# Expert layers of a routed network on one core: every third first-layer block in a third PSUM bank, and the next expert's weights converted in 14 small pieces

## The chip, the core and the metric

The kernel runs on one core of a Trainium2 chip. Its work is spread over the engines PE (TensorE, the matrix unit; its weight loads are listed apart as PEld), ACT (ScalarE), DVE (VectorE), POOL (GpSimd) and SP (SyncE, which here only issues transfers). The metric is the device time of one execution in microseconds (us). The kernel before takes 799.66 us, the median of three runs (799.56 to 800.76).

## What is computed

Three stages follow each other: a recurrent attention, a dense feed-forward layer, and a layer of eight experts. The change lies in the last one alone. Each of the 3072 tokens is given to one of 8 experts, 384 tokens to each, and passes through that expert's two matrices:

```
def _moe2_ref(x, w_gate, w1, w2):          # x 3072 x 384, w1 8 x 384 x 1024, w2 8 x 1024 x 384
    ...                                    # assigned[token] = expert, 384 tokens for each
    for e in range(E):
        mask = assigned == e
        h = np.maximum(x[mask] @ w1[e], 0.0)
        out[mask] = h @ w2[e]
```

## The kernel before

All matrices of the expert stage are multiplied as sums of f16 halves: a number is scaled and rounded to f16 (its high half), and what is left goes into a second f16 tile (its low half). A product of two such numbers takes three matmuls: high by high, high by low, low by high.

**One expert.** The loop over experts (L1223 to L1240) does the following for expert e.

- First layer, `e_mm1` (L1142 to L1163): the 1024 hidden features are cut into 8 blocks of 128. A block is 9 matmuls of 128 x 128 by 128 x 384 (3 slices of the 384 inputs, 3 products of halves each) into one PSUM tile `Hp`. ACT then writes the high half of its ReLU to `hT` (L1162), and DVE, which reads the same PSUM tile and ACT's result, writes the low half (L1163). Only after DVE has read it can the PSUM tile be filled again. `Hp` has two buffers, of one bank each, so block f waits until DVE is through with block f - 2. In expert 0 blocks 0 and 1 are worked on together, in three parts of 128 tokens, since their inputs come late.
- Behind each of the blocks 0 to 5 one step of the conversion of the next expert's weights is issued, `conv_w` (L1106): ACT writes the high half of a part of the staged f32 weights to `a` (L1101), DVE the low half (L1104). `halves` (L1089) sets the parts: three of 1024 elements per partition for w1, then two of 1152 and one of 768 for w2. Both tiles come from the staging tile `stg`, which SP fills for the expert after (L1084 for w1, L1086 for w2) as soon as DVE has read it.
- With block 0 POOL fetches the next expert's rows by index (`gather`, L1125).
- Second layer, `e_mm2` (L1168): three blocks of 128 tokens, 24 matmuls each (L1175). Ahead of each, PE transposes 128 of the next expert's rows (L1137), and ACT and DVE write their halves to `xe` (L1139, L1140). ACT scales the result (L1178) and POOL scatters it to the output (L1180).

Each engine takes its instructions in the order in which the program issues them, so on ACT and DVE the conversion of a part stands between the ReLU of a block and that of the next one. Expert 0's own weights are converted earlier, during the routing, by `small_pieces` (L1111): w1 in 6 pieces of 512 elements and w2 in 8 pieces of 384. The last expert, 7, has no weights to convert.

[...]

Of the kernel before, what the change touches and what calls it, by code (L numbers as in the profile page):

```python
# [9 lines left out]
F32 = mybir.dt.float32  # L10
# [8 lines left out]
P = 128  # L19
# [4 lines left out]
CFG = {'conv': [-28.559, -28.796, -9.197, -0.926, 0.696, 1.907, 2.814, 4.759, 2.932, 5.667, 6.934, 7.118, 8.281, 10.201,  # L24
          10.159, 10.891],
 'split': [-27.728, -26.98, -0.788, 1.233, 2.549, 2.564, 3.442, 5.926, 5.381, 6.383, 8.239, 9.176, 8.901, 10.848,
           10.815, 11.802],
 'ogT': [6.61, 8.484, 9.185, 9.828, 11.404, 11.777, 11.841, 12.734],
 'ogM': [8.421, 8.977, 10.284, 11.259, 11.757, 11.949, 12.856, 14.904],
 'u': ({'att0': -3.966,  # L30
        'bon1': -2.332,
        'bon2': -0.558,
# [122 lines left out]
 'alone': {9},  # L155
 'lg': 8.068,
 'hold': 30,
 'xq': set()}


@with_exitstack
def tile_rwkv_mish_greedy_moe(
# [17 lines left out]
    NE = w_gate.shape[1] * P // DM  # L180
# [11 lines left out]
    CAP = NT // NE  # L192
# [24 lines left out]
    pp = ctx.enter_context(tc.tile_pool(name="psm", bufs=1, space=PSUM))  # L217
# [560 lines left out]
    p_g2, p_g3, pgs = cms["g2"], cms["g3"], cms["ps"]  # L778
# [301 lines left out]
    NCV = KD + 3  # L1080

    def load_w(e):
        s1 = p2.tile([P, KD, F2], F32, name="stg")
        nc.sync.dma_start(s1.rearrange("p k f -> p (k f)"), w1[e])  # L1084
        s2 = p2.tile([P, NF2, DM], F32, name="stg")
        nc.sync.dma_start(s2.rearrange("p f d -> p (f d)"), w2[e])  # L1086
        wts[e] = (s1, s2)

    def halves(e, step):  # L1089
        s1, s2 = wts[e]  # L1090
        if step == 0:
            wf[e] = tuple(p2b[e % 2].tile(sh, F16, name=nm, bufs=1)
                          for sh, nm in (([P, 2, KD, F2], "a1"), ([P, 2, NF2, DM], "a2")))
        a1, a2 = wf[e]
        if step < KD:
            return s1[:, step], a1[:, :, step], SW1
        h = slice(3 * (step - KD), min(3 * (step - KD) + 3, NF2))
        return s2[:, h], a2[:, :, h], SW2

    def conv_hi(src, dst, sc_):  # L1100
        nc.scalar.activation(dst[:, 0], src, AF.Copy, scale=sc_)  # L1101

    def conv_lo(src, dst, sc_):
        nc.vector.scalar_tensor_tensor(dst[:, 1], src, sc_, dst[:, 0], op0=ALU.mult, op1=ALU.subtract)  # L1104

    def conv_w(e, step):  # L1106
        x = halves(e, step)
        conv_hi(*x)
        conv_lo(*x)

    def small_pieces(e):  # L1111
        for step in range(NCV):
            src, dst, sc_ = halves(e, step)
            if step < KD:
                for q in range(2):
                    c = slice(q * F2 // 2, (q + 1) * F2 // 2)
                    yield src[:, c], dst[:, :, c], sc_
            else:
                for q in range(src.shape[1]):
                    yield src[:, q], dst[:, :, q], sc_  # L1120

    def gather(e):
        for m in range(ME):
            t = xe[e, m] if (e, m) in xe else p3.tile([P, DM], F32, name="xr", bufs=4)
            nc.gpsimd.indirect_dma_start(  # L1125
                out=t, out_offset=None, in_=x1_dram[:, :],
                in_offset=bass.IndirectOffsetOnAxis(ap=idx[:, e * ME + m:e * ME + m + 1], axis=0))
            xe[e, m] = t

    def xpose(e, m):  # L1130
        if m == 0:
            xe[e] = p3.tile([P, 2, KD, CAP], F16, name="xe")
        x = xe[e]
        t = xe.pop((e, m))
        ps = pgs.tile([P, KD, P], F32, name="cn")
        for kk in range(KD):
            nc.tensor.transpose(ps[:, kk, :], t[:, kk * P:(kk + 1) * P], ident)  # L1137
        ms = slice(m * P, (m + 1) * P)
        nc.scalar.activation(x[:, 0, :, ms], ps, AF.Copy, scale=SX1)  # L1139
        nc.vector.scalar_tensor_tensor(x[:, 1, :, ms], ps, SX1, x[:, 0, :, ms], op0=ALU.mult, op1=ALU.subtract)  # L1140

    def e_mm1(e, *fs, parts=1):  # L1142
        a1, x = wf[e][0], xe.get(e)
        if 0 in fs:
            hT[e] = p3.tile([P, 2, NF2, CAP], F16, name="hT")
        h = hT[e]
        tiles = [pp.tile([P, CAP], F32, name="Hp", bufs=2) for _ in fs]
        for c in range(parts):
            cs = slice(c * CAP // parts, (c + 1) * CAP // parts)
            if parts > 1:  # L1150
                for m in range(c and c + 1, min(c + 2, parts)):
                    xpose(e, m)
                x = xe[e]
            for f, ps in zip(fs, tiles):
                n = 0
                for kk in range(KD):
                    for a, b in ((0, 0), (0, 1), (1, 0)):
                        nc.tensor.matmul(ps[:, cs], a1[:, a, kk, f * P:(f + 1) * P], x[:, b, kk, cs],  # L1158
                                         start=(n == 0), stop=(n == 3 * KD - 1))
                        n += 1  # L1160
        for f, ps in zip(fs, tiles):
            nc.scalar.activation(h[:, 0, f], ps, AF.Relu)  # L1162
            nc.vector.scalar_tensor_tensor(h[:, 1, f], ps, 0.0, h[:, 0, f], op0=ALU.max, op1=ALU.subtract)  # L1163
# [4 lines left out]
    def e_mm2(e, m):  # L1168
        a2, h = wf[e][1], hT[e]
        ps = pp.tile([P, DM], F32, name="X", bufs=2)  # L1170
        ms = slice(m * P, (m + 1) * P)
        n = 0
        for f in range(NF2):
            for a, b in ((0, 0), (0, 1), (1, 0)):
                nc.tensor.matmul(ps, h[:, a, f, ms], a2[:, b, f, :], start=(n == 0), stop=(n == 3 * NF2 - 1))  # L1175
                n += 1
        o = p3.tile([P, DM], F32, name="or", bufs=3)
        nc.scalar.activation(o, ps, AF.Copy, scale=1.0 / (SX1 * SW1 * SW2))  # L1178
        nc.gpsimd.memset(spacer, 0.0)  # L1179
        st_ = nc.gpsimd.indirect_dma_start(  # L1180
            out=out[:, :], out_offset=bass.IndirectOffsetOnAxis(ap=idx[:, e * ME + m:e * ME + m + 1], axis=0),
            in_=o, in_offset=None)
        for s_ in scat:
            tc.declare_no_dep(st_.ins, s_.ins, reason="each row is written once")
        scat.append(st_)
# [33 lines left out]
    if CFG["hold"]:  # L1219
        hold = pgs.tile([P, P], F32, name="cn")  # L1220
        for _ in range(CFG["hold"]):
            nc.tensor.matmul(hold[:, 0:P], ones, OH[:, 0], start=True, stop=True)  # L1222
    for e in range(NE):  # L1223
        nx = e + 1 < NE
        f = 0
        while f < NF2:
            k = 2 if e == 0 and f == 0 else 1
            e_mm1(e, *range(f, f + k), parts=ME if k > 1 else 1)
            for i in range(f, f + k):
                if i == 0 and nx:  # L1230
                    gather(e + 1)
                    if e > 0:
                        load_w(e + 1)
                if nx and i < NCV:
                    conv_w(e + 1, i)
            f += k
        for m in range(ME):
            if nx:
                xpose(e + 1, m)
            e_mm2(e, m)  # L1240
# [73 lines left out]
```

## Time and profile before

| | us |
|---|---|
| median of the runs | 799.66 |
| the profiled execution | 801.9 |
| its span, first to last instruction | 800.2 |
| PE busy | 748.7 (94%) |
| DVE busy | 546.7 (68%) |
| ACT busy | 457.3 (57%) |
| POOL busy | 58.7 (7%) |
| the expert stage in the span | 583.8 to the end |

The page of the profile cuts the span into 40 equal slices and gives the busy share of each engine in tenths. PE stands at 9 nearly throughout; the dip to 6 and 8 just behind the middle of the second half is the routing. Busy shares are averages over the span, and a PE that is 94% busy can still wait in one stage; that is read from the timeline of the stage, in which a bracket behind a row says how long the engine was idle before it and what ended the wait. Durations of matmuls include the time in the pipeline: a matmul of 384 columns shows 326 ns, though they follow each other more closely.

### The profile page before, as it was taken

What the parts mean: (1) busy time and instruction counts of PE and PEld (TensorE: products, weight loads), DVE (VectorE), ACT (ScalarE), POOL (GpSimd) and SP (SyncE); (2) the same over time, 40 slices, a digit from 0 to 9 for tenths busy, and PEclk for the clock granted to TensorE, in tenths of its full rate; (3) what the DMA queues carried; (4) which work ended last, traced back from release to release, by engine and by line L of the source; (5) the groups of instructions that cost most, each with busy time, mean ns of one, the idle gap of its engine ahead of it and who ended that gap; (6) DMA issues with size and microseconds to landing.
All of it is one profiled execution on the core that took longest, in us unless ns stands there. A gap on an engine that the chain in (4) does not pass through costs nothing. (4 is left out here: it accounts for less than half of the span.)

```text
span 800.2 us, 20251 instructions
## 1 busy us (share of the span) xinstructions
PE 748.7 (94%) x8848; PEld 519.3 (65%) x8848; DVE 546.7 (68%) x962; ACT 457.3 (57%) x711; POOL 58.7 (7%) x98
## 2 busy tenths in 40 slices
PE   5877789999999999999999999999689999999996
PEld 3465576877778777787877765555466555555563
DVE  7899995978879778796974556777653455335520
ACT  4369989686786877869686761110053455435521
POOL 0000000000000000000000010000112122312211
PEclk9799889999999999999999999999879999999999
DMA  9860521313223132231200032004224554355100
GB/s 342 247 187 19 157 71 27 72 44 77 51 56 81 28 84 53 56 81 27 52 16 16 2 124 75 22 11 137 77 86 160 198 196 146 127 184 207 50 30 29
DMA packets 22220, 74.12 MB, mean 93 GB/s; under 512 B 4496, under 2 KB 13072, under 8 KB 20080
## 3 DMA queue, kind: packets, MB, share of 16 engines
q1 hardware_dynamic: 19056, 63.35, 26.6%
q0 software_dynamic: 3072, 9.44, 3.7%
q8 instruction: 71, 1.16, 0.6%
q14 instruction: 21, 0.17, 0.1%
HBM read 62.15 MB, written 9.44 MB: 89 GB/s over the span
## 5 line engine op out<-in xcount | busy, mean ns | idle before, releaser
L570 PE MATMUL Hp<-xg,wi 128*128 128x256 f16 x1728 | 208.4, 277 | 0.4 <-DMA xg<-xg 0.3
L625 PE MATMUL X<-wo,g 128*128 128x392 f16 (+1 forms) x1152 | 208.4, 328 | 0.0
L570 PEld LDWEIGHTS <-wi 128*128 128x128 f16 x1728 | 167.2, 99 | 28.5 <-issue 0.9
L625 PEld LDWEIGHTS <-g 128*128 128x128 f16 x1152 | 107.1, 98 | 65.7 <-issue 0.9
L1158 PE MATMUL Hp<-xe,a 128*128 128x384 f16 (+1 forms) x612 | 102.2, 321 | 6.3 <-DVE hT L1163 5.2
L574 ACT ACTIVATE es<-Hp 128x512 f32<-128x512 f32 x96 | 57.0, 594 | 78.5 <-PE Hp L570 76.8
L1175 PE MATMUL X<-a,hT 128*128 128x384 f16 x576 | 97.2, 326 | 0.0
L1158 PEld LDWEIGHTS <-a 128*128 128x128 f16 x612 | 59.1, 100 | 48.2 <-issue 14.2
L1175 PEld LDWEIGHTS <-hT 128*128 128x128 f16 x576 | 56.4, 98 | 34.8
L597 DVE TENSOR_TENSOR hs<-hs,es 128x1024 f32<-128x1024 f32 x48 | 56.3, 1219 | 28.0 <-ACT es L589 27.9
L1163 DVE SCALAR_TENSOR_TENSOR hT<-Hp,hT 128x384 f16<-128x384 f32 x64 | 35.3, 553 | 47.3 <-ACT hT L1162 47.3
L610 DVE TENSOR_TENSOR g<-hs,g 128x1024 f16<-128x1024 f32 x48 | 58.4, 1223 | 6.7 <-ACT g L334 5.8
L1104 DVE SCALAR_TENSOR_TENSOR a<-stg,a 128x1024 f16<-128x1024 f32 (+4 forms) x56 | 59.6, 1066 | 3.2 <-ACT a L1101 2.7
L1178 ACT ACTIVATE or<-X 128x384 f32<-128x384 f32 x24 | 11.8, 490 | 81.0 <-issue 60.7
L1140 DVE SCALAR_TENSOR_TENSOR xe<-cn,xe 128x384 f16<-128x384 f32 x24 | 13.3, 555 | 63.2 <-ACT xe L1139 63.1
L334 ACT ACTIVATE x1o<-X 128x384 f32<-128x384 f32 x16 | 7.8, 490 | 81.9 <-PE X L625 52.0
L589 ACT ACTIVATE es<-es,right 128x1024 f32<-128x1024 f32 x48 | 51.8, 1139 | 0.2
L1101 ACT ACTIVATE a<-stg 128x1024 f16<-128x1024 f32 (+4 forms) x56 | 51.0, 926 | 1.0 <-DMA stg<-in_w_dram 1.0
L280 ACT ACT_TABLE_LOAD x39 | 50.0, 1283 | 1.5 <-PEq L1298 0.8
L1162 ACT ACTIVATE hT<-Hp 128x384 f16<-128x384 f32 x64 | 31.3, 490 | 33.3 <-PE Hp L1158 32.2
L582 ACT ACTIVATE es<-es,mid__124 128x2048 f32<-128x2048 f32 x24 | 48.0, 2002 | 0.1
L334 ACT ACTIVATE hs<-Hp 128x512 f32<-128x512 f32 x73 | 43.3, 592 | 0.0
(187 smaller groups left out, 879.3 us busy)
## 6 DMA issues: line engine op xcount, KB each, us to landing
stg<-in_w_dram SPq DMA_DIRECT2D x16, 1536.0 KB, 7.3
T<-in_rkw_dram SPq DMA_DIRECT2D x42, 289.5 KB, 4.9
g<-in_w_out_dram SPq DMA_DIRECT2D x8, 768.0 KB, 5.1
v<-in_v_dram SPq DMA_DIRECT2D x24, 192.0 KB, 2.4
x_dram<-x1o SPq DMA_DIRECT2D x48, 96.0 KB, 2.2
g<-in_w_in_dram SPq DMA_DIRECT2D x4, 768.0 KB, 8.2
wo<-in_w_in_dram SPq DMA_DIRECT2D x4, 768.0 KB, 13.2
xg<-xg SPq DMA_DIRECT2D x72, 16.0 KB, 1.8
```

What stands on the lines that cost most here:

```text
L280: nc.scalar.preload_act_table_set(sets[0])
L334: nc.scalar.activation(dst, src, AF.Copy, scale=scale)
L570: nc.tensor.matmul(h[:, fi, :], wi[:, a, kk, f * P:(f + 1) * P], xg[g][:, b, kk, :], start=(n == 0), stop=(n == 3 * KD - 1))
L574: nc.scalar.activation(es[g, hf][:, 2 * q:2 * q + 2, :], h, AF.Tanh, scale=0.5 / (SX * SWI))
L589: nc.scalar.activation(e, e, AF.Sin, scale=-2.0, bias=right)
L597: nc.vector.tensor_tensor(h, h, e, op=ALU.mult)
L610: (nc.vector if on_v("glo", 2 * H_ + q) else nc.gpsimd).tensor_tensor(gt[:, 1, sl], h, gt[:, 0, sl], op=ALU.subtract)
L625: nc.tensor.matmul(x, gt[:, a, ff, m * P:(m + 1) * P], wo[:, b, f, 0:n], start=(f == 0 and i == 0), stop=(f == NF - 1 and i == 2))
L1101: nc.scalar.activation(dst[:, 0], src, AF.Copy, scale=sc_)
L1104: nc.vector.scalar_tensor_tensor(dst[:, 1], src, sc_, dst[:, 0], op0=ALU.mult, op1=ALU.subtract)
L1158: nc.tensor.matmul(ps[:, cs], a1[:, a, kk, f * P:(f + 1) * P], x[:, b, kk, cs], start=(n == 0), stop=(n == 3 * KD - 1))
L1175: nc.tensor.matmul(ps, h[:, a, f, ms], a2[:, b, f, :], start=(n == 0), stop=(n == 3 * NF2 - 1))
```

## The change

The program takes two edits in the expert stage. Block f of the first layer with f % 3 == 2 (blocks 2 and 5) goes into a PSUM tile of its own, `hx`, with one buffer in the pool `pgs`; the other blocks keep the two buffers of `Hp`. And the weights of the next expert are converted in the 14 pieces of `small_pieces`, two behind each block, in place of the six steps of `conv_w`.

```
+ 'cvn': 2}
...
-        tiles = [pp.tile([P, CAP], F32, name="Hp", bufs=2) for _ in fs]
+        tiles = [pgs.tile([P, CAP], F32, name="hx", bufs=1) if f % 3 == 2 else pp.tile([P, CAP], F32, name="Hp", bufs=2)
+                 for f in fs]
...
+    pend = {}
+
+    def more_cv(e, n=None):
+        if e >= NE:
+            return
+        if e not in pend:
+            pend[e] = list(small_pieces(e))
+        for _ in range(n or CFG["cvn"]):
+            if pend[e]:
+                x = pend[e].pop(0)
+                conv_hi(*x)
+                conv_lo(*x)
+
...
-                if nx and i < NCV:
-                    conv_w(e + 1, i)
+                if nx:
+                    more_cv(e + 1)
             f += k
+        more_cv(e + 1, 100)
```

On DVE, in the first layer of expert 1, the program before has one row of conversion between the low halves of two blocks (`hT<-Hp` is the low half of a block, `a<-stg` the low half of a part of the next expert's weights, and the first row belongs to block 0):

```order
L1163 SCALAR_TENSOR_TENSOR hT<-Hp,hT 128x384 [waits Activation_49]
L1104 SCALAR_TENSOR_TENSOR a_11721<-stg,a_11721 128x1024 [waits DMAHW5_49,Activation_49]
L1163 SCALAR_TENSOR_TENSOR hT<-Hp,hT 128x384 [waits Activation_49]
L1104 SCALAR_TENSOR_TENSOR a_11721<-stg,a_11721 128x1024 [waits Activation_49]
L1163 SCALAR_TENSOR_TENSOR hT<-Hp,hT 128x384 [waits Activation_49]
L1104 SCALAR_TENSOR_TENSOR a_11721<-stg,a_11721 128x1024 [waits Activation_49]
L1163 SCALAR_TENSOR_TENSOR hT<-Hp,hT 128x384 [waits Activation_49]
L1104 SCALAR_TENSOR_TENSOR a_11722<-stg,a_11722 128x1152 [waits DMAHW6_49,PE_49,Activation_49]
L1163 SCALAR_TENSOR_TENSOR hT<-Hp,hT 128x384 [waits Activation_49]
```

The same place in the changed program has two rows of conversion in each gap, and blocks 2 and 5 read `hx`:

```order
L1165 SCALAR_TENSOR_TENSOR hT<-Hp,hT 128x384 [waits Activation_49]
L1105 SCALAR_TENSOR_TENSOR a_11737<-stg,a_11737 128x512 [waits DMAHW5_49,Activation_49]
L1105 SCALAR_TENSOR_TENSOR a_11737<-stg,a_11737 128x512 [waits Activation_49]
L1165 SCALAR_TENSOR_TENSOR hT<-Hp,hT 128x384 [waits Activation_49]
L1105 SCALAR_TENSOR_TENSOR a_11737<-stg,a_11737 128x512 [waits Activation_49] x2
L1165 SCALAR_TENSOR_TENSOR hT<-hx,hT 128x384 [waits Activation_49]
L1105 SCALAR_TENSOR_TENSOR a_11737<-stg,a_11737 128x512 [waits Activation_49] x2
L1165 SCALAR_TENSOR_TENSOR hT<-Hp,hT 128x384 [waits Activation_49]
L1105 SCALAR_TENSOR_TENSOR a_11738<-stg,a_11738 128x384 [waits DMAHW6_49,PE_49,Activation_49]
L1105 SCALAR_TENSOR_TENSOR a_11738<-stg,a_11738 128x384 [waits Activation_49]
L1165 SCALAR_TENSOR_TENSOR hT<-Hp,hT 128x384 [waits Activation_49]
L1105 SCALAR_TENSOR_TENSOR a_11738<-stg,a_11738 128x384 [waits Activation_49] x2
```

So up to block 5 the elements between two low halves go from 1024, 1024, 1024, 1152, 1152, 768 to 1024, 1024, 1024, 768, 768, 768, and a further 768 stand behind block 6; the order of the engines' other instructions is unchanged.

On PE, where block 2 of expert 1 begins, the program before has a wait on DVE at the block's first matmul (the first two rows are the end of block 1):

```order
L1158 LDWEIGHTS a_11506
L1158 MATMUL Hp<-xe,a_11506 128x384
L1158 LDWEIGHTS a_11506
L1158 MATMUL Hp<-xe,a_11506 128x384 [waits DVE_49]
L1158 LDWEIGHTS a_11506
L1158 MATMUL Hp<-xe,a_11506 128x384
```

In the changed program that matmul writes `hx`, whose last reader was a block of the expert before, and waits for nothing:

```order
L1160 LDWEIGHTS a_11506
L1160 MATMUL Hp<-xe,a_11506 128x384
L1160 LDWEIGHTS a_11506
L1160 MATMUL hx<-xe,a_11506 128x384
L1160 LDWEIGHTS a_11506
L1160 MATMUL hx<-xe,a_11506 128x384
```

The first matmul of each later block still waits on DVE, now for the block three before it, as the order of the buffers (Hp, Hp, hx, Hp, Hp, hx, Hp, Hp) gives it.

## Rows read from the trace of the kernel before

**Rows 1.** Waits of PE from 584 us on: us in all, times, longest.

```profile
PE Hp L1158 <- DVE hT L1163: 5.2, 15, 0.7
```

**Rows 2.** Windows, first layer (experts 1, 6, 7): length, PE, PEld, DVE, ACT, POOL, PEclk, DMA.

```profile
614.76:627.95 13.19, 12.46 (x75) 7.05 (x73) 10.34 (x13) 9.59 (x14) 4.98 (x5) 1.00 0.52 181
744.09:757.28 13.19, 12.46 (x75) 7.06 (x72) 10.34 (x13) 9.59 (x14) 4.93 (x5) 1.00 0.21 62
769.96:781.66 11.70, 11.70 (x74) 7.05 (x72) 3.90 (x7) 3.92 (x8) 1.05 (x2) 1.00 0.05 17
```

**Rows 3.** Timeline, first layer of expert 1: start, duration, engine, line; idle before.

```profile
616.43 0.49 ACT L1162 ACTIVATE hT<-Hp 128x384 f16<-128x384 f32 x1 [0.97 <-PE Hp L1158]
616.81 1.05 ACT L1101 ACTIVATE a<-stg 128x1024 f16<-128x1024 f32 x1
616.95 0.56 DVE L1163 SCALAR_TENSOR_TENSOR hT<-Hp,hT 128x384 f16<-128x384 f32 x1 [4.75 <-ACT hT L1162]
...
619.04 0.55 DVE L1163 SCALAR_TENSOR_TENSOR hT<-Hp,hT 128x384 f16<-128x384 f32 x1
...
619.51 1.22 DVE L1104 SCALAR_TENSOR_TENSOR a<-stg,a 128x1024 f16<-128x1024 f32 x1
619.64 4.82 PE L1158 MATMUL Hp<-xe,a 128*128 128x384 f16 x27 [0.33 <-DVE hT L1163]
...
620.64 0.55 DVE L1163 SCALAR_TENSOR_TENSOR hT<-Hp,hT 128x384 f16<-128x384 f32 x1
...
622.24 0.55 DVE L1163 SCALAR_TENSOR_TENSOR hT<-Hp,hT 128x384 f16<-128x384 f32 x1
...
624.15 0.55 DVE L1163 SCALAR_TENSOR_TENSOR hT<-Hp,hT 128x384 f16<-128x384 f32 x1
```

**Rows 4.** Timeline of DVE in the routing: small pieces, and what follows one.

```profile
494.82 0.69 DVE L1104 SCALAR_TENSOR_TENSOR a<-stg,a 128x512 f16<-128x512 f32 x1
495.45 0.15 DVE L867 TENSOR_TENSOR ge<-cn,remS 32x8 f16<-32x8 f32 x1
...
515.79 0.55 DVE L1104 SCALAR_TENSOR_TENSOR a<-stg,a 128x384 f16<-128x384 f32 x1
```

**Rows 5.** Timeline of ACT in the routing: small pieces back to back.

```profile
482.48 2.18 ACT L1101 ACTIVATE a<-stg 128x512 f16<-128x512 f32 x4
...
516.33 1.34 ACT L1101 ACTIVATE a<-stg 128x384 f16<-128x384 f32 x3
```

**Rows 6.** Timeline of expert 0's first layer: PE, and ACT and DVE behind block 0.

```profile
588.27 2.86 PE L1158 MATMUL Hp<-xe,a 128*128 128x128 f16 x36
...
591.24 1.02 DVE L1163 SCALAR_TENSOR_TENSOR hT<-Hp,hT 128x384 f16<-128x384 f32 x2 [1.65 <-ACT hT L1162]
591.55 1.99 ACT L1101 ACTIVATE a<-stg 128x1024 f16<-128x1024 f32 x2
591.86 3.08 PE L1158 MATMUL Hp<-xe,a 128*128 128x384 f16 x18 [0.73 <-DVE hT L1163]
...
602.08 0.49 PE L1137 MATMUL cn<-ident,xr 128*128 128x128 f32 x3
```

**Rows 7.** Timeline: first fetch of rows by POOL and its use, experts 0 and 1; others' queues.

```profile
576.72 1.13 POOL L1125 DMA_INDIRECT xr<-x_dram,idx  x1 [111.32 <-DVE idx L1076]
...
583.85 1.49 PE L1137 MATMUL cn<-ident,xr 128*128 128x128 f32 x6
...
617.00 0.99 POOL L1125 DMA_INDIRECT xr<-x_dram,idx  x1 [0.30 <-issue]
...
627.33 0.33 SPq L1086 DMA_DIRECT2D stg<-in_w_dram  x1
...
628.27 4.06 PE L1175 MATMUL X<-a,hT 128*128 128x384 f16 x24
```

**Rows 8.** DMA issues of the page: KB each, median us from issue to landing.

```profile
stg<-in_w_dram SPq DMA_DIRECT2D x16, 1536.0 KB, 7.3
```

More of the change, by code (lines that the diff above doesn't have):

```diff
@@ L157 @@
  'hold': 30,
- 'xq': set()}
+ 'xq': set(),
+ 'cvn': 2}
 @with_exitstack
```

## The prediction

> **What bounds the kernel now.** I read the page's busy shares first, then the waits of PE in the expert stage, then the windows of the first layers, then the timeline of one of them. PE is the engine that is busy nearly all the time, so only a pause of PE can be won back. In the expert stage nearly all of its waits are one kind: the matmuls of L1158 wait until DVE has read the PSUM tile that they are to fill again, 15 times, 5.2 us [rows 1]. That figure is too small: the profile models the ends of matmuls, and a matmul counts as busy while its result leaves the pipeline. The true size comes from comparing stages with equal matmul work. Expert 7 has no weights to convert, and its 72 first-layer matmuls take 11.70 us without a pause; the same 72 take 13.19 us in experts 1 and 6, and by the timeline in all six from 1 to 6 [rows 2]. So a pause-free block of 9 matmuls takes 11.70 / 8 = 1.46 us, 0.1625 us per matmul, and an expert loses 13.19 - 11.70 = 1.49 us. [...]
>
> DVE is busy 10.34 us of those 13.19 [rows 2], so it isn't the bound on average; it is the bound in the blocks that carry a conversion. From 619.04 on its rows show no wait in front of them: the low half of a block starts, the conversion starts 0.47 us behind it (619.04 to 619.51), and the next block's low half 1.13 us behind that (619.51 to 620.64) [rows 3]. That is 1.60 us per block of 1024 elements against 1.46 of PE, and 1.91 with 1152 elements (622.24 to 624.15). With two PSUM buffers PE follows at DVE's pace: the matmul at 619.64 starts 0.05 us after the low half of 619.04 ended (619.04 + 0.55).
>
> **The change, part by part.** The third bank lets block f wait for the low half of block f - 3 instead of f - 2. The pieces spread the conversion over seven blocks instead of six, at the cost of eight more instructions on ACT and on DVE per expert. I work the stage out in us from its first matmul, for an expert from 1 to 6, from the intervals of the rows.
>
> ACT: the ReLU starts 1.67 us after its block's first matmul (614.76 to 616.43) and holds ACT for 0.38 (to 616.81) [rows 2, 3]. A piece of 512 adds 0.52 when four follow each other ((2.18 - 0.62) / 3, the 0.62 being one whole piece), a piece of 384 adds 0.42 ((1.34 - 0.51) / 2) [rows 5]. Per block that is 0.38 + 1.04 = 1.42, then 0.38 + 0.84 = 1.22: below 1.46, so the ReLU is never late.
>
> DVE: a low half starts 0.52 us after its ReLU at the earliest (616.43 to 616.95), holds DVE for 0.47 and ends 0.55 after its start [rows 3]. A piece of 512 takes 0.63 until the next instruction starts (494.82 to 495.45). For 384 the row has only the duration, 0.55 [rows 4], equal to that of the low half of the same size; so I take that one's 0.47 and keep 0.55 as the upper end, which would add 8 x 0.08 = 0.64 us of DVE work per expert. A block thus costs DVE 0.47 + 2 x 0.63 = 1.73 us in blocks 0 to 2 and 0.47 + 2 x 0.47 = 1.41 in blocks 3 to 6. Block 0's low half starts at 1.67 + 0.52 = 2.19, its first piece at 2.70 (when ACT's is written: 1.67 + 0.38 + 0.62 + 0.03), so the low halves of blocks 1 to 4 start at 3.96, 5.69, 7.42, 8.83 and those of blocks 0 to 4 end at 2.74, 4.51, 6.24, 7.97 and 9.38. PE without pauses wants the buffers of blocks 3 to 7 0.05 us before 4.39, 5.85, 7.31, 8.78 and 10.24. Each is free in time, with 1.60, 1.29, 1.02, 0.76 and 0.81 us to spare. With 0.55 for a piece of 384 only the last of these shrinks, to 0.65 (block 4's low half is the first behind such pieces). All of the 1.49 us goes: 6 x 1.49 = 8.94 us.
>
> Expert 0 is worked out by itself, since its blocks 0 and 1 end together. Blocks 2 to 7 run from 591.86 to 602.08, 10.22 us, against 6 x 1.4625 = 8.78. Ahead of them PE waits 0.73 us for the low half of block 0 [rows 6], and as the last 128-column matmul (0.22 us long, 0.08 behind the one before) overlaps its follower by 0.14, block 2 could start 0.87 us earlier, at 590.99; in the changed program its tile is `hx`, which nobody holds. DVE then has two low halves from 591.24, and four pieces of 512 from 592.20 (591.55 + 0.62 + 0.03), so block 2's low half starts at 594.72 and ends at 595.27, in time for block 5 (595.38). Block 3's starts 0.47 + 1.26 later, at 596.45, and ends at 597.00; block 6 wants its tile at 596.79 and pauses 0.21. Block 7 follows without a pause and ends at 599.97. Gain: 602.08 - 599.97 = 2.11 us.
>
> What is late next? DVE ends block 7's low half at 13.6 us, and the second layer needs it for its last three matmuls of the first 24: 11.70 + 0.32 to its start (627.95 to 628.27) + 21 x 0.1625 = 15.4 [rows 2, 7]. 1.8 us to spare. POOL fetches the next rows 10.95 us before PE transposes them (617.00 to 627.95), 9.5 after the change; for expert 0, 7.13 us were enough (576.72 to 583.85) [rows 7]. SP refills the staging tile of w2 when DVE is through with the last piece: 12.57 us after the stage's start now (614.76 to 627.33), some 13.1 then, landing 7.3 us later [rows 7, 8] at 20.4; ACT wants it in block 3 of the next expert, at 24.4 + 6.4 = 30.8. No queue gets a new order but ACT's and DVE's, and behind the added waits stand only the same low halves that I counted.
>
> Sum: 8.94 + 2.11 = 11.05 us, off the profiled execution's 801.9 (span 800.2, 1.7 around it): 790.9. The runs' median is 2.2 us lower at 799.66, so I forecast 788.6.
>
> **Rivals.** (a) The third bank does not act, because `hx` waits like the tiles of the other pool or blocks 3, 4, 6 and 7 still find theirs held. With the pieces alone and two buffers, the same intervals let blocks 3, 4 and 5 start at 4.56, 6.29 and 8.02 (each 0.05 behind the low half two blocks before it), blocks 6 and 7 follow without a pause, and the stage ends at 12.40. Six experts gain 0.79 each, expert 0 (whose block 2 keeps its pause) about 0.8: 5.5 us, 794.1. For it: nothing in a trace of before shows `hx`. Against it: in the order of the instructions the first matmul of block 2 has no wait left.
>
> (b) The pieces cost more than the rows say. With d more per piece, the low half of block 4 ends at 9.38 + 8d against the 10.19 that block 7 wants, so pauses begin at d = 0.10; halfway, at d = 0.20, block 7 starts at 9.43 + 8d and the stage ends at 10.89 + 8 x 0.20 = 12.5 us, a gain of 0.7 per expert, some 5 in all: 794.5. For it: on DVE two pieces of 512 already cost 1.26 against 1.13 for 1024 at once. Against it: that is 0.07 a piece, and I have counted it.
>
> (c) The other side, by the same mechanism: from d = 0.29 the stage is longer than 13.19, as DVE's queue of 14 pieces decides its end in place of the buffers. At d = 0.4 it takes 10.89 + 3.2 = 14.09, 0.90 more in each of seven experts: 6.3 us slower, 806.0. Already at the turning point a piece of 512 would have to hold DVE for 0.92 us, against 0.63 in the row [rows 4].
> [...]
>
> (d) PE gains the pauses but the end does not move, since another engine's chain sets it: the chain of waits runs along POOL's scatter. Against it: POOL has 4.98 us of work in 13.19 [rows 2], and its scatter waits for results of PE. No change, 799.7.
>
> **How the numbers follow.** The forecast has 0.78, with a range of its own from 787.5 to 789.7, the scatter of the runs shown (799.56 to 800.76) and the 0.21 of expert 0 to either side. (a) has 0.07, (b) 0.08, (c) 0.03, (d) 0.04. What a measurement of this kernel can tell from no change is about 0.2%, 1.6 us. Faster are the forecast, (a) and (b): 0.93; same (d), 0.04; slower (c), 0.03. The range goes from 787.3 to 794.0, which takes in the forecast and half of (a) and (b).
>
> **What would show it.** In the profile after, the first layer of experts 1 to 6 takes 11.70 us, as expert 7's does, and PE waits for L1163's successor almost nowhere, save once in expert 0. DVE's rows of 512 and 384 elements follow each other by 0.63 and 0.47. The second layers keep their length. A first layer of 12.4 us with pauses at blocks 3 to 5 would mean (a); pauses at blocks 6 and 7 alone, (b). The prediction is wrong if the first layers shrink and the median doesn't follow by the same sum, or if a pause turns up ahead of the second layer.

## The result and the profile after

The changed kernel takes 789.54 us (median of four runs, 788.59 to 791.47) against 800.21 for the kernel before beside it (799.56 to 802.31): a ratio of 0.9865, 95% interval 0.9838 to 0.9893, or 10.7 us. The forecast was 788.6.

In the expert stage the list of PE's waits has no wait for L1163's successor (L1165) any more. This is the list from 584 us on in the profile after (us, times, longest), to be set against [rows 1]; what is left is expert 0's wait for its first inputs:

```profile
PE Hp L1160 <- DVE xe L1141: 0.3, 1, 0.3
```

The windows of the first layers of experts 1, 6 and 7 in the profile after (columns as in [rows 2]):

```profile
610.83:622.53 11.70, 11.70 (x74) 7.09 (x72) 9.51 (x19) 10.08 (x22) 4.69 (x5) 1.00 0.50 162
732.74:744.44 11.70, 11.70 (x74) 7.09 (x72) 9.51 (x19) 10.08 (x22) 4.63 (x5) 1.00 0.23 69
757.13:768.83 11.70, 11.70 (x74) 7.04 (x73) 3.91 (x7) 3.93 (x8) 1.05 (x2) 1.00 0.05 17
```

The three are alike now, with the conversion (experts 1 and 6) and without (7). ACT is busy for 10.08 us instead of 9.59, for the added instructions; DVE's figure falls, 9.51 against 10.34, since the last two pieces lie behind the window's end. The timeline of expert 1 shows how (start, duration, engine, line; rows between left out):

```profile
613.02 0.56 DVE L1165 SCALAR_TENSOR_TENSOR hT<-Hp,hT 128x384 f16<-128x384 f32 x1 [4.75 <-ACT hT L1164]
...
614.75 0.55 DVE L1165 SCALAR_TENSOR_TENSOR hT<-Hp,hT 128x384 f16<-128x384 f32 x1
615.21 1.28 DVE L1105 SCALAR_TENSOR_TENSOR a<-stg,a 128x512 f16<-128x512 f32 x2
615.22 3.09 PE L1160 MATMUL Hp<-xe,a 128*128 128x384 f16 x18
...
616.41 0.55 DVE L1165 SCALAR_TENSOR_TENSOR hT<-hx,hT 128x384 f16<-128x384 f32 x1
...
618.08 0.56 DVE L1165 SCALAR_TENSOR_TENSOR hT<-Hp,hT 128x384 f16<-128x384 f32 x1
...
619.48 0.56 DVE L1165 SCALAR_TENSOR_TENSOR hT<-Hp,hT 128x384 f16<-128x384 f32 x1
...
622.75 1.03 DVE L1105 SCALAR_TENSOR_TENSOR a<-stg,a 128x384 f16<-128x384 f32 x2
...
623.68 0.56 DVE L1165 SCALAR_TENSOR_TENSOR hT<-Hp,hT 128x384 f16<-128x384 f32 x1
623.80 0.33 SPq L1087 DMA_DIRECT2D stg<-in_w_dram  x1
```

Counted from the stage's first matmul (610.83), the low halves of blocks 0 to 4 end at 2.75, 4.47, 6.13, 7.81 and 9.21 us, that of block 7 at 13.41. The row 615.22 holds blocks 3 and 4, and the first of them starts on time, 4.39 us in, though DVE is only at block 1's low half.

Expert 0 in the profile after, PE from its last group of 128-column matmuls to the second layer, beside [rows 6]:

```profile
586.97 2.48 PE L1160 MATMUL Hp<-xe,a 128*128 128x128 f16 x36
589.29 1.63 PE L1160 MATMUL hx<-xe,a 128*128 128x384 f16 x9
590.76 3.09 PE L1160 MATMUL Hp<-xe,a 128*128 128x384 f16 x18
593.68 1.63 PE L1160 MATMUL hx<-xe,a 128*128 128x384 f16 x9
595.23 3.09 PE L1160 MATMUL Hp<-xe,a 128*128 128x384 f16 x18
598.15 0.49 PE L1138 MATMUL cn<-ident,xr 128*128 128x128 f32 x3
```

From the first row to the last are 11.18 us, against 13.81 before (588.27 to 602.08): 2.63 us. With 6 x 1.49 = 8.94 that is 11.57 us, of the 12.8 between the two spans (800.2 and 787.4). The other 1.2 us lie ahead of these rows (their first matmul starts at 588.27 and at 586.97), where the two programs are the same; over the profiles of the experiments below, that start falls anywhere from 585.14 to 588.46. So the runs' 10.7 us and the stage's 11.6 agree within what varies ahead of the stage.

### The profile page after: what moved, and what is told of

The parts are those of the page before. It is cut to its first block, busy times and chain, and to the rows that moved or that the text cites. A ratio compares the mean times of both kernels' runs of the same rounds, so it can differ in the third digit from the quotient of the medians.

```text
span 787.4 us, 20363 instructions
## 1 busy us (share of the span) xinstructions
PE 744.8 (95%) x8848; PEld 519.8 (66%) x8848; DVE 548.9 (70%) x1018; ACT 461.0 (59%) x767; POOL 57.0 (7%) x98
## 3 DMA queue, kind: packets, MB, share of 16 engines
q8 instruction: 71, 1.16, 0.6%
## 5 line engine op out<-in xcount | busy, mean ns | idle before, releaser
L1160 PE MATMUL Hp<-xe,a 128*128 128x384 f16 (+1 forms) x468 | 75.8, 318 | 0.3 <-DVE xe L1141 0.3
L1105 DVE SCALAR_TENSOR_TENSOR a<-stg,a 128x384 f16<-128x384 f32 (+1 forms) x112 | 64.1, 611 | 0.0
L1102 ACT ACTIVATE a<-stg 128x384 f16<-128x384 f32 (+1 forms) x112 | 56.9, 562 | 0.7 <-DMA stg<-in_w_dram 0.7
L1165 DVE SCALAR_TENSOR_TENSOR hT<-Hp,hT 128x384 f16<-128x384 f32 x48 | 26.6, 556 | 38.8 <-ACT hT L1164 38.8
L1126 POOL DMA_INDIRECT xr<-x_dram,idx x24 | 27.5, 1146 | 121.1 <-DVE idx L1077 111.3
## 6 DMA issues: line engine op xcount, KB each, us to landing
wo<-in_w_in_dram SPq DMA_DIRECT2D x4, 768.0 KB, 11.6
```

The source lines that it names most:

```text
L1126: nc.gpsimd.indirect_dma_start(out=t, out_offset=None, in_=x1_dram[:, :], in_offset=bass.IndirectOffsetOnAxis(ap=idx[:, e * ME + m:e * ME ...
```

## The experiments

Theory A: PE's pauses come from a PSUM tile that DVE has not read yet, and the third tile takes them away by itself; the small pieces matter little. Theory B: the small pieces do it, as no low half stands behind a long conversion any more. All runs are compared with the kernel before on the same chip, the first four on one and the last three on another.

**The third bank alone.** Only the tiles are changed; `conv_w` and its six large steps stay.

```
-        tiles = [pp.tile([P, CAP], F32, name="Hp", bufs=2) for _ in fs]
+        tiles = [pgs.tile([P, CAP], F32, name="hx", bufs=1) if f % 3 == 2 else pp.tile([P, CAP], F32, name="Hp", bufs=2)
+                 for f in fs]
```

> The third bank alone, conversions left in their six large steps. Theory A (PE's pauses come from a PSUM tile that DVE has not read yet, and a third tile alone covers DVE's lag): the low halves of blocks 0 to 4 end at 2.75, 4.83, 6.43, 8.03 and 9.94 us after the stage's start in the trace of before, all ahead of the 4.39, 5.85, 7.31, 8.78 and 10.24 at which blocks 3 to 7 want the tiles, so the first layers of experts 1 to 6 take 11.70 us as with both edits; expert 0 pauses some 0.5 us more than with both. Time within 1 us of the kernel with both edits, some 10.5 us below before. Theory B (the small pieces do most of it, since they keep ACT and DVE from standing behind a long instruction): the first layers stay at 12.4 us or more and the gain is at most half.

790.00 us against 801.61, ratio 0.9866 (0.9844 to 0.9888): the whole gain as far as these runs can tell, as A has it. The window of expert 1's first layer, and DVE's low halves of its blocks 1, 3 and 4 there:

```profile
610.65:622.35 11.70, 11.70 (x74) 7.09 (x73) 9.13 (x12) 9.44 (x14) 4.98 (x5) 1.00 0.48 154
```

```profile
614.92 0.55 DVE L1164 SCALAR_TENSOR_TENSOR hT<-Hp,hT 128x384 f16<-128x384 f32 x1
...
618.12 0.55 DVE L1164 SCALAR_TENSOR_TENSOR hT<-Hp,hT 128x384 f16<-128x384 f32 x1
...
619.85 0.55 DVE L1164 SCALAR_TENSOR_TENSOR hT<-Hp,hT 128x384 f16<-128x384 f32 x1
```

The first two start 4.27 and 7.47 us after the stage does; before it was 4.28 and 7.48 (619.04 and 622.24 less 614.76 [rows 2, 3]). Up to block 3 DVE is as late as ever; PE has only stopped waiting for it. In expert 0 the pieces do add something: from the 36 matmuls of 128 columns to the second layer the timeline has 11.62 us here (586.34 to 597.96), 0.44 more than the 11.18 with both edits.

**The pieces alone.** The changed kernel with `hx` taken out again.

```
-        tiles = [pgs.tile([P, CAP], F32, name="hx", bufs=1) if f % 3 == 2 else pp.tile([P, CAP], F32, name="Hp", bufs=2)
-                 for f in fs]
+        tiles = [pp.tile([P, CAP], F32, name="Hp", bufs=2) for _ in fs]
```

> The 14 small pieces alone, all blocks in the two buffers of Hp. Theory A: pauses remain in blocks 3 to 5; the first layers of experts 1 to 6 take 12.2 to 12.4 us (as rival (a) of the prediction works out), a gain of 5 to 6.5 us against before. Theory B: 11.7 to 11.9 us, nearly the whole gain. If the pieces do nothing by themselves: 13.2 us and no gain.

794.29 us, ratio 0.9914 (0.9897 to 0.9932), some 7 us: between A's 5 to 6.5 and B's whole gain, and the first layers say which. Expert 1's, window and the PE row of the timeline (its first row), with the next row of PE and, between them, DVE's low half of block 3:

```profile
613.49:625.73 12.24, 12.15 (x74) 7.07 (x72) 10.05 (x20) 10.14 (x22) 4.70 (x5) 1.00 0.52 177
```

```profile
613.49 12.40 PE L1159 MATMUL Hp<-xe,a 128*128 128x384 f16 x72
...
620.75 0.55 DVE L1164 SCALAR_TENSOR_TENSOR hT<-Hp,hT 128x384 f16<-128x384 f32 x1
...
625.73 0.49 PE L1138 MATMUL cn<-ident,xr 128*128 128x128 f32 x3
```

12.24 us, within A's 12.2 to 12.4: the pieces take 0.95 of the 1.49 us, and 0.54 stay. Note how little of the pause a profile shows: the 72 matmuls stand in one row without a gap. A matmul of 384 columns is shown as 0.326 us long, though the next can start 0.1625 behind it (11.70 / 72), so a pause below the 0.16 between the two isn't idle time to the profile; one sees it only as 12.40 where the same 72, in the next experiment, take 11.86 in one row.

**Late conversions, two banks.** The kernel before with its six steps moved out of the first layer, three ahead of each of the first two token blocks of the second layer.

```
-                if nx and i < NCV:
-                    conv_w(e + 1, i)
...
             if nx:
                 xpose(e + 1, m)
+                for i in range(3 * m, min(3 * m + 3, NCV)):
+                    conv_w(e + 1, i)
             e_mm2(e, m)
```

> Two buffers of Hp and the six large steps, but three of them issued ahead of each of the first two token blocks of the second layer instead of behind the blocks of the first layer. Theory A, in its full form (a tile is held only because a conversion stands on DVE between two low halves): the first layers take 11.70 us with two buffers, the second layers keep 12.68 us (DVE and ACT have over 3 us of idle time per token block there); expert 0 still waits some 0.9 us for the low half of block 0. Gain some 10 us. If two buffers are too few in themselves, the first layers stay above 11.9 us; if the conversions delay the second layer's results or the next expert's inputs, the second layers grow.

789.76 us, ratio 0.9848 (0.9823 to 0.9873): the gain without a third bank. Expert 1, windows of the first and the second layer, and the one row of the first layer's matmuls:

```profile
612.14:623.84 11.70, 11.70 (x74) 7.09 (x72) 3.90 (x7) 3.92 (x8) 3.94 (x5) 1.00 0.52 192
623.84:636.53 12.69, 12.69 (x84) 8.08 (x82) 8.95 (x10) 8.28 (x12) 2.63 (x4) 1.00 0.44 161
```

```profile
612.14 11.86 PE L1158 MATMUL Hp<-xe,a 128*128 128x384 f16 x72
```

Two buffers are enough where nothing stands between two low halves, and the second layer, 12.69 us, holds the conversions for nothing. So the pause before had two conditions, the conversion in DVE's queue and only two tiles; to lift either one is enough. That holds for experts 1 to 6; in expert 0, where the low halves of blocks 0 and 1 follow each other, two tiles still cost the pause ahead of block 2, as expected:

```profile
PE Hp L1158 <- DVE hT L1163: 0.7, 1, 0.7
```

**The changed kernel again.**

> The changed kernel once more, beside the others on the same chip. First layers of 11.70 us, time 10 to 11 us below before. [...]

788.89 us, ratio 0.9851 (0.9829 to 0.9873). The stretch of 128-column matmuls in expert 0 differs from execution to execution of the same kernel. Here the granted clock is 1.00 over the last 36 of them (their 2.36 us hold a wait of 0.19 for `xe`); in the first profile after, the mean over them was 0.86. The 17 matmuls earlier take 1.41 us here and 1.97 there, where the granted clock ahead of the 36 was 0.50. The window of the 36 and the row of the 17 of this run, then the window ahead of the 36 and the row of the 17 of the first profile after:

```profile
586.17:588.53 2.36, 2.17 (x38) 2.04 (x36) 0.56 (x1) 0.73 (x2) 0.00 (x0) 1.00 0.30 87
```

```profile
584.59 1.41 PE L1160 MATMUL Hp<-xe,a 128*128 128x128 f16 x17 [0.33 <-DVE xe L1141]
```

```profile
582.55:586.97 4.42, 4.09 (x29) 3.66 (x28) 1.12 (x2) 0.98 (x2) 1.97 (x3) 0.50 0.25 68
```

```profile
584.57 1.97 PE L1160 MATMUL Hp<-xe,a 128*128 128x128 f16 x17 [0.33 <-DVE xe L1141]
```

The intervals of this kernel, the bank alone and the late conversions overlap; these runs can't order the three.

**Smaller pieces.** With the third bank, each of the 14 pieces cut in two, four behind each block (28), or in four, eight behind each block (56; n is a quarter there, and 'cvn' 8).

```
+    def tiny_pieces(e):
+        for src, dst, sc_ in small_pieces(e):
+            n = src.shape[1] // 2
+            for q in range(2):
+                yield src[:, q * n:(q + 1) * n], dst[:, :, q * n:(q + 1) * n], sc_
...
- 'cvn': 2}
+ 'cvn': 4}
...
-            pend[e] = list(small_pieces(e))
+            pend[e] = list(tiny_pieces(e))
```

> Third bank as changed, every small piece cut in two: 12 of 256 elements and 16 of 192 per expert, four behind each block. From the intervals of the profile after (512 elements 0.60 us, 384 elements 0.47 to the next instruction on DVE, so some 0.08 fixed and 1.02 ns per element) a block costs DVE 0.47 + 4 x 0.34 = 1.83 us, then 0.47 + 4 x 0.275 = 1.57. Theory A with this fixed cost: block 4's low half ends at 9.80 us, before the 10.19 at which block 7 wants its tile, so first layers of 11.70 us and no change of the time against the kernel with 14 pieces (within 1 us). [...]

> Third bank as changed, every small piece cut in four: 24 of 128 elements and 32 of 96, eight behind each block. With 0.08 us fixed a block costs DVE 0.47 + 8 x 0.21 = 2.15 us, then 0.47 + 8 x 0.18 = 1.91; the low halves of blocks 3 and 4 end at 9.2 and 11.1 us, too late for blocks 6 and 7 (8.73 and 10.19), and that of block 7 at 16.8, too late for the last three of the second layer's first 24 matmuls (16.3). First layers of 12.6 us, second layers some 0.5 longer: 1.4 us in each of seven experts, about 10 us in all, which gives back the whole gain (close to the time before). That is rival (c) of the prediction, made to happen. [...] If DVE's queue doesn't set the pace at all, 11.70 us as with 14 pieces.

28 pieces: 790.11 us, ratio 0.9881 (0.9862 to 0.9901), first layer of expert 1 unchanged but for 0.01. 56 pieces: 794.49 against 799.81, ratio 0.9932 (0.9913 to 0.9951): about half of the gain given back, not all of it as expected. The windows of expert 1's first layer, with 28 and with 56:

```profile
609.41:621.12 11.71, 11.71 (x75) 7.09 (x73) 9.52 (x29) 10.53 (x35) 4.24 (x5) 1.00 0.48 156
```

```profile
614.03:626.34 12.31, 12.02 (x73) 7.08 (x72) 10.12 (x46) 11.14 (x52) 4.04 (x5) 1.00 0.46 139
```

With 56, DVE's row from one low half to the next in blocks 0 and 4, and the PE rows of blocks 5 to 7, of the same expert:

```profile
616.22 0.56 DVE L1171 SCALAR_TENSOR_TENSOR hT<-Hp,hT 128x384 f16<-128x384 f32 x1 [4.75 <-ACT hT L1170]
...
618.30 0.56 DVE L1171 SCALAR_TENSOR_TENSOR hT<-Hp,hT 128x384 f16<-128x384 f32 x1
...
621.34 1.63 PE L1166 MATMUL hx<-xe,a 128*128 128x384 f16 x9
...
623.07 1.62 PE L1166 MATMUL Hp<-xe,a 128*128 128x384 f16 x9
...
624.26 0.57 DVE L1171 SCALAR_TENSOR_TENSOR hT<-Hp,hT 128x384 f16<-128x384 f32 x1
...
624.88 1.62 PE L1166 MATMUL Hp<-xe,a 128*128 128x384 f16 x9 [0.19 <-DVE hT L1171]
...
626.07 0.57 DVE L1171 SCALAR_TENSOR_TENSOR hT<-hx,hT 128x384 f16<-128x384 f32 x1
```

Eight pieces of 128 take 618.30 - 616.22 - 0.47 = 1.61 us, 0.201 each, and eight of 96 take 626.07 - 624.26 - 0.47 = 1.34, 0.168 each: 1.05 ns per element and 0.07 us fixed. I had put the fixed part at 0.08 from two sizes that lie close together, and over the 32 pieces ahead of block 4's low half the difference decides: it ends 10.80 us into the stage (624.26 + 0.57 - 614.03), not 11.1. The second layer of this expert keeps its 12.68 us (626.34 to 639.02 by the timeline): block 7's low half, which ends at 630.27, is read only by the last of the first 24 matmuls (`e_mm2` takes the high half twice, then the low one), some 630.4 by 626.67 + 23 x 0.1625, and not by the last three as expected. PE pauses at blocks 6 and 7 alone, for 0.27 and 0.35 us (621.34 to 623.07 and 623.07 to 624.88, each less 1.46). So the pace of DVE's queue sets in between 28 and 56 pieces, with the sign that the prediction gave for (b); the end of (c), a first layer above 13.19 us, no run reached.

**Both ways at once.** The late conversions with the tiles of the third bank.

> Third bank, and the six large steps in the second layers (both ways of taking the pauses away at once). Theory A: nothing is left to win in experts 1 to 6, since PE has no pause in the first layers with either: 11.70 us. In expert 0 the pause ahead of block 2 (0.73 us by the profile's row with late conversions and two buffers) goes, and so do the small pauses of the large steps. Time within 0.3 us of the kernel with both edits, 0.9 us below late conversions alone: no difference that the runs can tell. If the two gains added up, it would be some 10 us lower still.

789.96 us, ratio 0.9881 (0.9861 to 0.9901). Expert 1's first layer takes 11.70 us again (611.11 to 622.81 by the timeline). The gains do not add up: there is one pause, and it can be taken away once. No version beat the changed kernel by anything that these runs can tell.

## Why the prediction was right

By its own steps:

- **The pause per expert.** Forecast 13.19 to 11.70 us in experts 1 to 6, 8.94 us in all; measured 11.70 in each. To take the size from expert 7, which does the same matmuls with nothing to convert, and not from the wait list's 5.2 us, was the step that made the number.
- **The recurrence on DVE.** Low halves forecast to end at 2.74, 4.51, 6.24, 7.97 and 9.38; measured 2.75, 4.47, 6.13, 7.81 and 9.21. The growing difference is the piece of 512: 0.60 us to the next instruction (615.21 to 616.41 for two) instead of the 0.63 read from the routing, where the follower reads `cn`, whose matmuls on PE end only at 495.42 (494.96 + 0.46 in the row below). The 384s took the 0.47 that I chose: 619.48 - 618.08 = 1.40 per block.

```profile
494.96 0.46 PE L853 MATMUL cn<-Eo,I__6985 128*32 128x8 f16 x12 [0.17 <-DVE I__6985 L848]
```

- **A misreading without a part in the sum.** The 1.91 us for a block of 1152 elements before is not DVE's own pace. The conversion at 622.88 starts 0.64 us behind the low half of 622.24, not 0.47, as it waits for ACT's half (621.69 + 1.16 = 622.85), and ACT was late since PE had paused ahead of that block. With the bank alone the same step takes 1.73 us (618.12 to 619.85). So part of the pauses before came from earlier pauses.

```profile
621.69 1.16 ACT L1101 ACTIVATE a<-stg 128x1152 f16<-128x1152 f32 x1
...
622.88 1.36 DVE L1104 SCALAR_TENSOR_TENSOR a<-stg,a 128x1152 f16<-128x1152 f32 x1
```

- **What is late next.** Block 7's low half was to end at 13.6 and w2's staging to be refilled at 13.1: 13.41 and 12.97. The limit of 15.4 was set too early, as only the last of the three matmuls named there reads the low half, but nothing hung on it. No other queue became the bound, and the second layers kept 12.7 us.
- **Expert 0** was the mis-sized term: 2.11 forecast, 2.63 measured. 0.12 is the pause of block 6, 0.09 us (593.68 + 1.46 to 595.23) instead of 0.21, by the cheaper pieces. The other 0.40 is the stretch of 128-column matmuls ahead of block 2: 2.32 us in the profile after, where I had kept the 2.72 of before. In the profiles before and after, the granted clock goes from 0.50 in the 4.42 us ahead of these matmuls (583.85 to 588.27 before, 582.55 to 586.97 after) to 1.00 behind them (590.90 to 592.00 and 589.29 to 590.80), and its mean over them differs from execution to execution (0.86 and 1.00 in the two of the changed kernel). Before, after and in the run with the pieces alone, from the first of these 36 matmuls on:

```profile
588.27:590.90 2.63, 2.63 (x36) 2.63 (x35) 0.56 (x1) 0.67 (x2) 0.00 (x0) 0.73 0.12 48
```

```profile
586.97:589.29 2.32, 2.32 (x37) 2.31 (x36) 0.56 (x1) 0.73 (x2) 0.00 (x0) 0.86 0.12 48
```

```profile
588.22:590.66 2.44, 2.33 (x38) 2.09 (x36) 0.56 (x1) 0.90 (x2) 0.00 (x0) 1.00 0.14 54
```

  The column behind POOL is the granted clock, as a mean over the window: 0.73, 0.86 and 1.00. The rows of the 36 matmuls are 2.86, 2.48 and 2.44 us long. The last run has two banks as the kernel before has, so the 0.40 us do not go with the third bank; that they go with the clock is my estimate from these three rows. They are luck, as are the 1.2 us ahead of these matmuls: without both, the two profiles differ by 11.2 us, near the 11.05 forecast and the 10.7 of the runs.
- **The rivals.** (a) was worked out at 12.40 us for the pieces with two banks; made to happen, they gave 12.24, by the cheaper pieces again (block 3's low half ends at 620.75 + 0.55 - 613.49 = 7.81 instead of 7.97). (b) and (c) needed 0.10 and 0.29 us more per piece; those of 512 were 0.03 cheaper than the rows said and those of 384 as chosen. (d) fell with the end following the first layers.

What the prediction left out is that in experts 1 to 6 the small pieces were not needed: its own list of times held the proof, as the low halves of before (up to 9.94 us for block 4, 624.15 + 0.55 - 614.76 [rows 2, 3]) already end ahead of what three banks ask for (10.19). I worked out the pieces without the bank and both together, not the bank without the pieces.

## What to carry to other kernels

Where a busy engine pauses for a buffer, lay out when each reader is through and when each writer wants the buffer: here one more buffer was worth the lags that fell between the two, and nothing where every lag was covered already. Take the size of short PE pauses from a stage with the same matmuls and nothing else to do, not from the wait list, which here showed 5.2 of some 11 us. If there is no bank to spare, move the work that delays the reader to a stage where its engine is idle, which here gave the same gain.

## What the runs showed of the hardware

An added small instruction was cheaper here than its duration suggests. On DVE a piece costs 0.07 us and 1.05 ns per element from start to start down to 96 elements, though the profile shows 0.27 us for such a one. On ACT eight pieces of 128 elements take 1.69 us and eight of 96 take 1.49 in these rows of the run with 56 pieces, the single one 0.30 and 0.29 long. The groups of the pieces (the second number behind the bar is the mean ns of one) and the two rows of ACT:

```profile
L1102 ACT ACTIVATE a<-stg 128x96 f16<-128x96 f32 x192 | 35.9, 287 | 0.0
L1105 DVE SCALAR_TENSOR_TENSOR a<-stg,a 128x96 f16<-128x96 f32 x192 | 34.8, 273 | 0.0
...
L1102 ACT ACTIVATE a<-stg 128x128 f16<-128x128 f32 x144 | 30.6, 302 | 0.0
```

```profile
616.08 1.69 ACT L1102 ACTIVATE a<-stg 128x128 f16<-128x128 f32 x8
...
623.73 1.49 ACT L1102 ACTIVATE a<-stg 128x96 f16<-128x96 f32 x8
```

That is (1.69 - 0.30) / 7 = 0.199 and (1.49 - 0.29) / 7 = 0.171 us from start to start, 0.9 ns per element and 0.09 us fixed. The fixed part of the durations is somewhat more than twice that: 0.273 - 96 x 1.05 ns = 0.17 us on DVE, where the queue showed 0.07, and 0.29 - 96 x 0.9 ns = 0.20 us on ACT.
